# A recurrent attention block in front of two MLPs: another order for the first block, fewer products for the key grams, other kinds of products for the joins

## The chip, the cores and the metric

The kernel runs on one core of a Trainium2 chip. The metric is device time in microseconds. One core has five engines that run side by side and meet only at semaphores: TensorE (PE) multiplies matrices, VectorE (DVE) and ScalarE (ACT) work elementwise and empty PSUM, GpSimd (POOL) does a few elementwise jobs, SyncE (SP) issues the DMAs.

## The reference, cut to what matters

Attention with a delta rule over 768 steps for 32 (batch, head) pairs with head dimension 48, then two MLPs of 384 by 2048, the first with ELU, the second with a sigmoid gate.

```python
k_n = k / (norm(k, axis=-1) + 1e-06)
for t in range(S):
    y[:, :, t] = einsum('bhd,bhde->bhe', q[:, :, t], state)
    v_old = einsum('bhde,bhd->bhe', state, k_n[:, :, t])
    state = state + beta[:, :, t] * einsum('bhd,bhe->bhde', k_n[:, :, t], v[:, :, t] - v_old)
x = y.transpose(0, 2, 1, 3).reshape(B * S, H * D)
h = x @ w_in                                   # first MLP
x = where(h > 0, h, exp(minimum(h, 0)) - 1) @ w_out
h = x @ w_in2                                  # second MLP
out = (h * sigmoid(1.702 * h)) @ w_out2
```

## The kernel before, in words

The 768 steps are cut into six blocks of 128 tokens (`p`, 0 to 5), each of two chunks of 64 (`c = 2p` and `2p + 1`). Within a chunk the recurrence is solved by the inverse of a triangular matrix that is built from the products of the keys.

Two kinds of work share PE. The MLPs run as 192 *units*: two layers, six blocks of tokens, 16 slices `m` of the hidden dimension. A unit's nine products into `h` (`up`, L699) give 128 hidden values for 512 tokens; two units later nine products into `acc` (`down`, L736) take them further. Both kinds are fp32r, 512 columns wide, with each operand split in a high and a low part. The attention of block p+1 is laid between the units of block p of the first layer. Only the attention of block 0 has nothing to hide behind: it stands in front of the first unit and is called the *head* here. Its end is the first row of L699.

The attention's steps, with the names that the text uses:

- **gram** (L196 in later blocks, L210 in the first two): products of the keys of a chunk, into PSUM tile `ps_w`, from there to `z` in SBUF. L196 makes them in pieces of 32 rows, so that the two halves of each row piece come out already swapped; one ACT copy (L202) empties them.
- **inverse**: a chain of small VectorE steps (`take`, `root`, `norm` with L300, `scale` L304, 14 `rows` of L320 and L325 each, `finish`, `turn`). `also(n)` puts n steps of block 1's inverse between the steps of the head; what is left of them goes into the first units by `spread`.
- **join** (`join16`; `left` L360 or L376, `right` L360 or L389): puts the inverses of 16 by 16 together to 32 by 32, in products of 64 by 64 with a block-diagonal operand (`pairs`, L360) or in four times as many of 32 by 32 or 16 by 32 (L376, L389). `block` (L345) copies the block-diagonal operand.
- **kq**, **mask** (L492), **t2**, **m1** (L508), **m2** (L523, L434), **ks** (L539), **w** (L556), **state** (L579), **y** (near part L604, far part L614): the rest of a chunk, in this order of need. `state` of a chunk feeds `ks` of the next one, `ks` feeds `w`, and `y` gives the MLP's input `xh`, `xl`.
- **weight steps** (`bases` L658, `conv`: shift L665, rest L668, cast L675, low L679): turn a loaded slice of weights into its high and low part. Unit m needs slice m.

All of it is a manual schedule: every engine runs its instructions in the order in which the code issues them, and waits in place. `ps_w` is a single PSUM tile of two banks, so each use of it waits until the one before has been copied out. In the unit loop the places of a unit are called `fill` (behind ACT's first two operations), `mid` (ahead of the unit's second VectorE operation) and `end` (behind the cast L721 of the unit); a *slot* 2u is mid of unit u, 2u + 1 is its end. Weight slice m + 2 stands in `fill` of unit m.

Of the kernel before, what the change touches and what calls it, by code (L numbers as in the profile page):

```python
# [31 lines left out]
class Kernel:  # L32
# [34 lines left out]
    def constants(self):  # L67
# [6 lines left out]
        for c in range(2):  # L74
            t = self.wp.tile([P, 2 * DM, 2], F32, name="raw", tag="wt").rearrange("p k i -> p (k i)")[:, 0:1024]
            nc.gpsimd.memset(t, 0.0)
            self.blocks.append(t.rearrange("p (u t) -> p u t", u=16))
# [15 lines left out]
        for k in range(2):  # L93
            for turn in range(2):
                t = self.ap.tile([P, 2, HS], F32, name=f"su{k}{turn}")
                nc.gpsimd.memset(t, 0.0)
                self.su[k, turn] = t
        self.x1d = self.dp.tile([NP, P, NK, TB], F32, name="x1d")
# [83 lines left out]
    def gram(self, c, kt, ps=None):  # L182

        s = self.pas[c // 2]
        if ps is None:
            both = self.wide()
            ps = [both[:, hf] for hf in range(2)]
# [9 lines left out]
        z = s["z"][:, 16 * (c % 2):16 * (c % 2) + 16, :].rearrange("p (f u) t -> p f (u t)", f=2)  # L197
        if c < 2:
            self.nc.scalar.copy(z[:, 0], ps[0])
            self.nc.vector.tensor_copy(z[:, 1], ps[1])  # L200
        else:
            self.nc.scalar.copy(z, both)  # L202

    def gram64(self, c, kt, ps):
# [6 lines left out]

        z = self.pas[c // 2]["z"][:, 16 * (c % 2):16 * (c % 2) + 16, :]
# [134 lines left out]
    def join16(self, c, home):  # L347
# [5 lines left out]
        wide = [c < 4, 0 < c < 4]  # L353

        def pairs(ps, x, half):

            for u in range(8 * half, 8 * half + 8):
                for o in (0, 64):
                    r = slice(o, o + 64)
                    pe.matmul(ps[r, u, :], own["d"][r, u, :], x[r, u, :], start=True, stop=True)  # L360
# [5 lines left out]
        def left(half):  # L366
# [3 lines left out]
            if wide[0]:  # L370
                own["d"] = self.blocks[c % 2 if c < 2 else 1 - c % 2]
                pairs(ps, s["zt"][:, us, 16:32], half)
# [7 lines left out]
        def right(half):  # L380
# [3 lines left out]
            if wide[1]:  # L384
                pairs(ps, own["ys"], half)
# [8 lines left out]
        def blocked():  # L394
            if wide[1]:
                own["d"] = self.blocks[0 if c == 1 else 1 - c % 2]
                self.block(own["d"], own["t1"])
# [45 lines left out]
    def chunk(self, c):  # L443
# [144 lines left out]
        def y():  # L588
            self.x_tiles(("a", c // 2))
            xh, xl = self.x["a", c // 2]  # L590
            if self.early:
                ps = [self.bank(True) for _ in range(2)]
            else:
                both = self.wide()
                ps = [both[:, i] for i in range(2)]
            for i in range(2):
                for ab in range(2):
                    t = 64 * (2 * i + ab)
                    for hf in range(2):
                        k = self.w_half(hf, ab)  # L600
                        for j in range(4):
                            u = 4 * i + j
                            d = 64 * u + 16 * (u % 2)
                            pe.matmul(  # L604
                                ps[0][32 * j:32 * j + 32, 256 * hf + t:256 * hf + t + 64], su[k][:, hf, d:d + 32],
                                g["x"][k][:, 8 * hf + u, :], start=True, stop=True,
                            )
                    for odd in range(2):
                        for hf in range(2):
                            k = self.w_half(hf, ab)  # L610
                            for j in range(2):
                                u, r = 4 * i + 2 * j + odd, 64 * hf + 32 * j
                                d = 64 * u - 16 if odd else 64 * u + 32
                                pe.matmul(  # L614
                                    ps[1][r:r + 32, t:t + 64], su[k][:, hf, d:d + 32], g["x"][k][:, 8 * hf + u, :],
                                    start=not odd, stop=odd == 1,
                                )
            dst = slice(256 * (c % 2), 256 * (c % 2) + 256)
            if self.early:
                pieces = [(slice(0, 2), ps[0]), (slice(2, 3), ps[1][:, 0:256])]  # L620
            else:
                pieces = [(slice(0, 3), both.rearrange("p i t -> p (i t)")[:, 0:768])]
            for r, src in pieces:
                src = src.rearrange("p (k t) -> p k t", t=256)
                act.copy(xh[:, r, dst], src)
# [563 lines left out]
```

## Time and profile before

| | us |
|---|---|
| median of 3 runs | 994.9 (994.07 to 996.52) |
| profiled execution | 994.21 |
| its span, first to last instruction | 992.5 |
| PE busy | 951.7 (96%) |
| DVE busy | 598.2 (60%) |
| ACT busy | 455.6 (46%) |

The shares are means over unlike stretches. From 200 us on PE is busy to within one or two per cent in every stretch; in front of the first unit (73.4 us) it is not, and DVE and ACT are busier there than later. A wait that counts is one of PE behind the head, or one on the chain that leads up to the first unit.

### The profile page before, as it was taken

Reading aid. Unit: us, or ns where it says so; the run is one execution under the profiler, and the core shown is the slowest. Engines: PE = TensorE matmul, PEld = TensorE weight load, DVE = VectorE, ACT = ScalarE, POOL = GpSimd, SP = SyncE. Lnnn points to the kernel's source line nnn. Section 1 sums busy time; section 2 is a strip of 40 time slices with the busy share of each in tenths; the row PEclk is TensorE's granted clock in tenths of the full one; section 3 lists DMA queues with packets and bytes.
Section 4 is the critical chain, followed back from the end, with each engine's and each line's share of the span. In section 5 each row is a group of like instructions: output and inputs, shape, how many; then the busy total and the mean of one; then the engine's idle time right before and its main releaser. Section 6 shows DMA issues by size and latency. Waiting matters only on the chain.

```text
span 992.5 us, 26270 instructions
## 1 busy us (share of the span) xinstructions
PE 951.7 (96%) x11840; PEld 782.4 (79%) x11840; DVE 598.2 (60%) x1038; ACT 455.6 (46%) x754; POOL 80.2 (8%) x71
## 2 busy tenths in 40 slices
PE   4689979999999999999999999999999999999998
PEld 4677767878878887887887888888888888888886
DVE  6878789577886887886445766733333333333332
ACT  6556656443445445444446675533333233333322
POOL 3112222010001001000000100100001001010000
PEclk9999989999999999999999999999999999999999
DMA  7154341502312130210104901010010010100000
GB/s 229 78 194 146 99 144 41 171 5 78 96 56 77 54 98 19 85 51 34 35 19 158 396 1 64 1 40 25 0 64 1 1 64 1 64 0 1 33 1 32
DMA packets 20177, 68.38 MB, mean 69 GB/s; under 512 B 3168, under 2 KB 4704, under 8 KB 20064
## 3 DMA queue, kind: packets, MB, share of 16 engines
q1 hardware_dynamic: 19920, 66.56, 19.6%
q8 instruction: 93, 1.52, 0.6%
q14 instruction: 20, 0.16, 0.1%
q10 hardware_dynamic: 144, 0.13, 0.0%
HBM read 57.25 MB, written 9.44 MB: 67 GB/s over the span
## 4 chain that ended last, share of the span: by engine, by line
PE 88%; DVE 5%; ACT 3%; issue 2%; DMA 1%; POOL 0%; SPq 0%; ACTq 0%; POOLq 0%; DVEq 0%
PE h L699 39%; PE acc L736 28%; PE accn L736 10%; PE ps_w L196 1%; PE ps_w L481 1%; PE ps_w L539 1%; PE ps_b L360 1%; PE ps_w L604 1%; PE ps_w L556 1%; PE ps_w L614 1%; DVE w L665 1%; DMA kg<-in_kT 1%; PE ps_w L579 1%; DVE w L668 1%; PE ps_w L434 1%
## 5 line engine op out<-in xcount | busy, mean ns | idle before, releaser
L699 PE MATMUL h<-xh,wt 128*128 128x512 f32 x1152 | 394.2, 396 | 1.2 <-DVE xl L626 1.2
L736 PE MATMUL acc<-gh,wt 128*128 128x512 f32 x864 | 293.2, 394 | 0.5 <-DVE xo L797 0.5
L699 PEld LDWEIGHTS h<-xh,wt 128*128 128x128 f32 x1152 | 217.0, 188 | 49.4 <-DVE xl L626 1.4
L699 PE MATMUL h<-xl,wt 128*128 128x512 f32 x576 | 225.1, 391 | 0.0
L721 ACT CAST gh<-t 128x512 fp32r<-128x512 f32 x192 | 119.3, 621 | 181.1 <-DVE t L712 125.0
L736 PEld LDWEIGHTS acc<-gh,wt 128*128 128x128 f32 x864 | 163.0, 189 | 36.1 <-issue 1.4
L724 DVE TENSOR_TENSOR gl<-t,gh 128x512 fp32r<-128x512 f32 x192 | 138.6, 722 | 71.4 <-ACT gh L721 71.3
L736 PE MATMUL acc<-gl,wt 128*128 128x512 f32 x432 | 169.0, 391 | 0.0
L718 DVE TENSOR_TENSOR t<-t,h 128x512 f32<-128x512 f32 x96 | 66.0, 688 | 168.8 <-ACT t L715 168.7
L715 ACT ACTIVATE t<-h 128x512 f32<-128x512 f32 x96 | 57.5, 599 | 187.3 <-PE h L699 187.3
L699 PEld LDWEIGHTS h<-xl,wt 128*128 128x128 f32 x576 | 108.7, 189 | 21.1
L712 DVE SCALAR_TENSOR_TENSOR t<-t,h 128x512 f32<-128x512 f32 x96 | 65.7, 684 | 65.4 <-ACT t L709 65.0
L708 ACT ACTIVATE t<-h 128x512 f32<-128x512 f32 x96 | 57.5, 598 | 89.6 <-PE h L699 88.9
L736 PE MATMUL accn<-gh,wt 128*128 128x512 f32 x288 | 96.4, 389 | 0.0
L736 PEld LDWEIGHTS acc<-gl,wt 128*128 128x128 f32 x432 | 81.6, 189 | 16.2
L736 PEld LDWEIGHTS accn<-gh,wt 128*128 128x128 f32 x288 | 54.1, 188 | 11.2
L709 ACT ACTIVATE t<-t 128x512 f32<-128x512 f32 x96 | 60.7, 632 | 3.1
L763 POOL TENSOR_TENSOR xl<-x1r,xh 128x512 fp32r<-128x512 f32 x18 | 24.1, 1337 | 408.3 <-ACT xh L762 314.4
L736 PE MATMUL accn<-gl,wt 128*128 128x512 f32 x144 | 56.0, 389 | 0.0
L492 DVE TENSOR_TENSOR x<-ps_w,mask_p 64x512 f32<-64x512 f32 x44 | 30.2, 687 | 12.6 <-PE ps_w L481 12.1
L679 POOL TENSOR_TENSOR wt<-w,wt 128x768 fp32r<-128x768 f32 x16 | 29.4, 1841 | 65.8 <-ACT wt L675 65.7
L668 DVE SCALAR_TENSOR_TENSOR w<-raw,w 128x768 uint32<-128x768 uint32 x32 | 33.7, 1053 | 0.9
(181 smaller groups left out, 857.6 us busy)
## 6 DMA issues: line engine op xcount, KB each, us to landing
raw<-in_w SPq DMA_DIRECT2D x32, 768.0 KB, 7.7
kt<-in_kT SPq DMA_DIRECT2D x12, 512.0 KB, 4.3
x<-in_qT SPq DMA_DIRECT2D x24, 256.0 KB, 4.1
kg<-in_kT SPq DMA_DIRECT2D x9, 512.0 KB, 5.0
kn<-in_kn SPq DMA_DIRECT2D x12, 384.0 KB, 3.5
x1d<-xo SPq DMA_DIRECT2D x12, 384.0 KB, 2.9
x1r<-x1d SPq DMA_DIRECT2D x6, 768.0 KB, 4.7
vn<-in_vn SPq DMA_DIRECT2D x11, 384.0 KB, 3.6
```

Source lines behind the costliest of these rows:

```text
L492: v.tensor_tensor(out=g["x"][k][self.tok(k), 8 * hf:8 * hf + 8], in0=i, in1=self.mask_p[t].unsqueeze(1).to_broadcast(list(i.shape)), op=AL ...
L668: v.scalar_tensor_tensor(out=bits[m], in0=words(m, 0), scalar=29, in1=bits[m], op0=ALU.logical_shift_right, op1=ALU.bitwise_or)
L679: (v if layer else nc.gpsimd).tensor_tensor(out=wt[:, 1], in0=bits.pop(m).bitcast(F32), in1=wt[:, 0].bitcast(F32), op=ALU.subtract)
L699: nc.tensor.matmul(hps, wt[:, part, k * P:(k + 1) * P], src[:, k], start=(i == 0), stop=(i == 3 * NK - 1))
L708: nc.scalar.activation(out=t, in_=hps, func=AF.Relu, scale=-1.0)
L709: nc.scalar.activation(out=t, in_=t, func=AF.Exp, scale=-1.0)
L712: nc.vector.scalar_tensor_tensor(out=t, in0=t, scalar=-1.0, in1=hps, op0=ALU.add, op1=ALU.max)
L715: nc.scalar.activation(out=t, in_=hps, func=AF.Sigmoid, scale=1.702)
L718: nc.vector.tensor_tensor(out=t, in0=t, in1=hps, op=ALU.mult)
L721: nc.scalar.copy(gh, t)
L724: nc.vector.tensor_tensor(out=gl, in0=t, in1=gh.bitcast(F32), op=ALU.subtract)
L736: self.nc.tensor.matmul(self.acc[c], wt[:, part, DM + c * P:DM + (c + 1) * P], src, start=(m == 0 and i == 0), stop=(m == NM - 1 and i == 2),)
```

## The change

Five edits.

1. **Gram of blocks 2 to 5**: 32 products of 64 rows instead of 64 of 32 rows. The halves now come out unswapped, so two more ACT copies of 32 partitions by 1024 (L192 of the changed kernel) swap them on the way out.
2. **Joins**: chunk 0's right part becomes a product by pairs like the other three of block 0 (a third block-diagonal operand, four more small ACT copies). Chunks 2 and 3 go the other way: four times as many small products, and no block copies.
3. **Head**: another order of the same steps. All four masks of chunk 0 move ahead of block 1's `take`; chunk 0's right join comes ahead of the weight steps; 13 of block 1's 23 inverse steps stand in the head instead of 21; the state of chunk 0 goes into `acc` banks instead of `h`.
4. **y in two parts**: `ya` and `yb`. In the head the near part of chunk 0's y stands ahead of ks of chunk 1, the far part behind it.
5. **Slots in the units**: the grams of block 2 move from end of units 1 and 3 to mid of units 0 and 1, state of chunk 1 from mid of unit 0 to mid of unit 2, most steps of chunks 2 and 3 one or two slots back; y of chunk 2 from mid of unit 9 to mid of unit 10; the first gram of block 3 from end of unit 13 (right behind y of chunk 3) to end of unit 14.

```diff
-    def gram(self, c, kt, ps=None):
...
-        for u in range(8):
-            for hf, ab in self.order():
-                r = 64 * self.s_half(hf, ab)
-                k = kt[r:r + D, 8 * hf + u, :]
-                o = ps[hf][:, 64 * u:64 * u + 64]
-                turned = kt[r:r + D, 8 * hf + u, :].rearrange("p (a b) -> p a b", a=2)[:, ::-1]
-                for sub, x in ((0, k), (1, turned)):
-                    q = 64 * ab + 32 * sub
-                    self.nc.tensor.matmul(o[q:q + 32], k[:, 32 * sub:32 * sub + 32], x, start=True, stop=True)
...
+    def gram(self, c, kt):
+
+        both = self.wide()
+        self.gram_products(kt, [both[:, hf] for hf in range(2)])
+        z = self.pas[c // 2]["z"][:, 16 * (c % 2):16 * (c % 2) + 16, :]
+        x = both.rearrange("p f (u t) -> p (f u) t", u=8)
+        self.nc.scalar.copy(z, x)
+        for r in (slice(32, 64), slice(96, 128)):
+            self.nc.scalar.copy(z[r].rearrange("p u (a b) -> p u a b", a=2), x[r].rearrange("p u (a b) -> p u a b", a=2)[:, :, ::-1])
+
+    def gram_products(self, kt, ps):
...
                 self.nc.tensor.matmul(ps[hf][64 * ab:64 * ab + 64, 64 * u:64 * u + 64], k, k, start=True, stop=True)
...
-        wide = [c < 4, 0 < c < 4]
+        wide = [c < 2, c < 2]
...
             if first:
-                ps = [self.bank(True) for _ in range(2)]
+                ps = self.banks(0)
...
+        run(j0[0], j1[0])
+        run(j0[3], j0[1], j0[2])
+        run(j1[1], j1[3], j1[2])
+        c0["mask"]()
+        also(2)
+        run(j0[4], j0[5], bases[0], c0["t2"])
+        also(1)
+        run(bases[1], c0["m1"], conv[0], conv[1], c0["nv"])
+        run(j1[4], j1[5], c1["t2"])
+        run(c0["m2"], c1["mask"], c1["m1"], conv[2], c0["ks"], c0["w"], conv[3])
+        run(bases[2], c1["m2"], c1["nv"])
+        c0["state"]()
...
+        also(2)
+        run(c0["ya"], c1["ks"], c0["yb"], bases[3])
+        also(2)
+        run(conv[4], c1["w"])
         nc.scalar.activation(out=self.one, in_=self.one, func=AF.Exp)
...
+        also(6)
+        run(c1["ya"], c1["yb"])
...
-            spread(fill, 0, 2, [f for _, f in beside], [size for size, _ in beside])
+            spread(fill, 0, 3, [f for _, f in beside], [size for size, _ in beside])
...
-                self.passes(at, spread, end, fill, p, (1, 3), (6, o + 2), lambda: turned(2))
+                self.passes(at, spread, (mid, end), fill, p, (0, 2), (6, o + 2), lambda: turned(2))
```

What moved, at two places that the prediction speaks of. VectorE between chunk 1's w and the first unit, before (L563 copies chunk 1's w, L320 and L325 are rows of block 1's inverse, L626 writes the first unit's `xl`, L329 to L336 finish the inverse, L665 and L668 prepare weight slice 2):

```order
L563 COPY su_93<-acc_1028 64x8x48
L320 TENSOR_TENSOR tmp<-W 128x72
L325 TENSOR_TENSOR W<-W,tmp 128x2x3x12
...
L626 TENSOR_TENSOR xl<-h,xh 128x2x256
L626 TENSOR_TENSOR xl<-h,xh 128x256
L329 MEMSET W 128x32
L330 TENSOR_TENSOR W<-W,f 128x1024
L336 STREAM_TRANSPOSE xl<-W 128x32x32
L665 TENSOR_SCALAR w<-raw 128x768
L668 SCALAR_TENSOR_TENSOR w<-raw,w 128x768
```

The same stretch in the changed kernel (L297 is `scale`, L554 the copy of w, L313 and L318 the rows, L624 `xl`, L682 and L685 weight slice 2):

```order
L297 TENSOR_TENSOR W<-W,na 128x1024
L554 COPY su_90<-acc_975 64x8x48
L554 COPY su_94<-acc_975 64x8x48
L313 TENSOR_TENSOR tmp<-W 128x28
...
L624 TENSOR_TENSOR xl<-h,xh 128x2x256
L624 TENSOR_TENSOR xl<-h,xh 128x256
L313 TENSOR_TENSOR tmp<-W 128x112
...
L318 TENSOR_TENSOR W<-W,tmp 128x2x3x12
L682 TENSOR_SCALAR w<-raw 128x768
L685 SCALAR_TENSOR_TENSOR w<-raw,w 128x768
```

`scale` now stands in front of the copy of w, six rows stand between that copy and `xl`, and six more between `xl` and weight slice 2; the finish of the inverse is behind that slice.

ScalarE in the unit that holds the first gram of block 2, before (unit 1: L675 casts a weight slice, L721 casts `gh`, L202 empties the gram, L658 and L653 belong to later slices, L708 and L709 open the next unit):

```order
L675 CAST wt<-w 128x768
L721 CAST gh<-t 128x512
L202 COPY z<-ps_w 128x1024
L658 ACTIVATE raw<-raw 128x768
L653 COPY raw<-one 128x1
L708 ACTIVATE t<-h 128x512
L709 ACTIVATE t<-t 128x512
```

In the changed kernel (unit 0: L692 casts the weight slice, L190 and L192 empty the gram, L738 casts `gh`, L675 and L670 belong to later slices, L725 and L726 open the next unit):

```order
L692 CAST wt<-w 128x768
L190 COPY z<-ps_w 128x1024
L192 COPY z<-ps_w 32x1024 x2
L738 CAST gh<-t 128x512
L675 ACTIVATE raw<-raw 128x768
L670 COPY raw<-one 128x1
L725 ACTIVATE t<-h 128x512
L726 ACTIVATE t<-t 128x512
L692 CAST wt<-w 128x768
```

Three copies stand ahead of the cast of `gh` where one stood behind it, and the second gram's three copies follow one unit later.

## Rows read from the trace of the kernel before

**Rows 1.** The page: busy time with instruction counts; the instruction queue (packets, MB, share).

```profile
PE 951.7 (96%) x11840; PEld 782.4 (79%) x11840; DVE 598.2 (60%) x1038; ACT 455.6 (46%) x754; POOL 80.2 (8%) x71
...
q8 instruction: 93, 1.52, 0.6%
```

**Rows 2.** Waits of PE: us in total, times, longest.

```profile
PE ps_w L614 <- issue: 4.4, 1, 4.4
...
PE ps_w L196 <- DVE xl L626: 2.4, 1, 2.4
```

**Rows 3.** Timeline of PE, head and first units: start, us, instruction [idle before].

```profile
28.55 3.60 PE L360 MATMUL h<-xl,raw 64*64 64x16 f32 x64 [3.13 <-DVE xl L336]
...
53.50 2.02 PE L579 MATMUL h<-su,kn 64*48 64x48 f32 x64
...
57.87 2.45 PE L539 MATMUL ps_w<-su,kt 48*64 48x48 f32 x64 [0.51 <-ACT su L795]
...
73.41 0.50 PE L699 MATMUL h<-xh,wt 128*128 128x512 f32 x1 [1.22 <-DVE xl L626]
...
90.28 1.16 PE L481 MATMUL ps_w<-x,kt 48*64 48x64 f32 x64
...
93.64 2.04 PE L360 MATMUL ps_b<-xh,raw 64*64 64x16 f32 x64
...
97.88 1.58 PE L196 MATMUL ps_w<-kg 48*32 48x64 f32 x128
99.39 0.50 PE L699 MATMUL h<-xh,wt 128*128 128x512 f32 x1
```

**Rows 4.** Timeline of DVE, head and unit 0.

```profile
20.98 0.28 DVE L325 TENSOR_TENSOR W<-W,tmp 128x112 f32<-128x112 f32 x1
...
38.47 0.42 DVE L392 TENSOR_TENSOR z<-xl,h 128x256 f32<-128x256 f32 x1
...
42.22 0.18 DVE L300 TENSOR_SCALAR na<-f 128x32 f32<-128x32 f32 x1
...
45.14 1.23 DVE L304 TENSOR_TENSOR W<-W,na 128x1024 f32<-128x1024 f32 x1
...
76.96 0.55 DVE L665 TENSOR_SCALAR w<-raw 128x768 uint32<-128x768 uint32 x1
77.54 0.96 DVE L668 SCALAR_TENSOR_TENSOR w<-raw,w 128x768 uint32<-128x768 uint32 x1
```

**Rows 5.** Groups of ACT by form: busy us, mean ns of one, idle before.

```profile
L721 ACT CAST gh<-t 128x512 fp32r<-128x512 f32 x192 | 119.3, 621 | 181.1 <-DVE t L712 125.0 <-DVE t L718 55.7
L709 ACT ACTIVATE t<-t 128x512 f32<-128x512 f32 x96 | 60.7, 632 | 3.1
...
L708 ACT ACTIVATE t<-h 128x512 f32<-128x512 f32 x96 | 57.5, 598 | 89.6 <-PE h L699 88.9
L658 ACT ACTIVATE raw<-raw 128x768 f32<-128x768 f32 x32 | 28.8, 909 | 0.4 <-DMA raw<-in_w 0.2
L675 ACT CAST wt<-w 128x768 fp32r<-128x768 f32 x32 | 26.4, 825 | 9.8 <-DVE w L668 9.8
...
L437 ACT ACTIVATE z<-ps_w 32x1024 f32<-32x1024 f32 x10 | 10.2, 1018 | 5.7 <-PE ps_w L434 5.6
L202 ACT COPY z<-ps_w 128x1024 f32<-128x1024 f32 x8 | 8.1, 1012 | 3.0 <-PE ps_w L196 3.0
```

**Rows 6.** Timeline of ACT in the head.

```profile
57.35 0.97 ACT L795 COPY su<-h 48x384 f32<-48x384 f32 x2
58.22 1.20 ACT L528 ACTIVATE z<-ps_b 32x512 f32<-32x512 f32 x2
```

**Rows 7.** Timeline of PE: behind chunk 2's y, and a join by quarters.

```profile
141.87 0.48 PE L614 MATMUL ps_w<-x,su 128*32 128x64 f32 x9 [4.41 <-issue]
...
209.49 1.26 PE L389 MATMUL ps_b<-w 16*32 16x16 f32 x128
```

**Rows 8.** Windows: us, busy (x) of PE, PEld, DVE, ACT, POOL, granted clock, DMA share, GB/s.

```profile
142.00:146.00 4.00, 4.00 (x18) 3.06 (x17) 2.86 (x5) 1.99 (x3) 0.00 (x0) 0.50 0.02 4
```

More of the change, by code (lines that the diff above doesn't have):

```diff
@@ L97, in constants @@
                 self.su[k, turn] = t
+        nc.gpsimd.memset(self.blocks[2], 0.0)
         self.x1d = self.dp.tile([NP, P, NK, TB], F32, name="x1d")
@@ L370, in left @@
             if wide[0]:
-                own["d"] = self.blocks[c % 2 if c < 2 else 1 - c % 2]
-                pairs(ps, s["zt"][:, us, 16:32], half)
+                pairs(ps, self.blocks[c], s["zt"][:, us, 16:32], half)
             for u in range(8 * half, 8 * half + 8 * (not wide[0])):
@@ L384, in right @@
             if wide[1]:
-                pairs(ps, own["ys"], half)
+                pairs(ps, self.blocks[2 - 2 * c], own["ys"], half)
             for u in range(8 * half, 8 * half + 8 * (not wide[1])):
@@ new lines, in y_near @@
+        def y_near(i):
+            ps = st["y"]
+            for ab in range(2):
+                t = 64 * (2 * i + ab)
+                for hf in range(2):
+                    k = self.w_half(hf, ab)
+                    for j in range(4):
+                        u = 4 * i + j
+                        d = 64 * u + 16 * (u % 2)
+                        pe.matmul(
+                            ps[0][32 * j:32 * j + 32, 256 * hf + t:256 * hf + t + 64], su[k][:, hf, d:d + 32],
+                            g["x"][k][:, 8 * hf + u, :], start=True, stop=True,
+                        )
@@ L618, in y, with y_out @@
-            dst = slice(256 * (c % 2), 256 * (c % 2) + 256)
+                                ps[1][r:r + 32, t:t + 64], su[k][:, hf, d:d + 32], g["x"][k][:, 8 * hf + u, :],
+                                start=not odd, stop=odd == 1,
+                            )
+        def y_out(r, src):
+            xh, xl = self.x["a", c // 2]
+            dst = slice(256 * (c % 2), 256 * (c % 2) + 256)
+            src = src.rearrange("p (k t) -> p k t", t=256)
+            act.copy(xh[:, r, dst], src)
+            v.tensor_tensor(out=xl[:, r, dst], in0=src, in1=xh[:, r, dst].bitcast(F32), op=ALU.subtract)
@@ L619, in y, with ya @@
+        def ya():
+            y_tiles()
+            y_near(0)
             if self.early:
-                pieces = [(slice(0, 2), ps[0]), (slice(2, 3), ps[1][:, 0:256])]
-            else:
[L622 to L625, printed above, removed]
-                v.tensor_tensor(out=xl[:, r, dst], in0=src, in1=xh[:, r, dst].bitcast(F32), op=ALU.subtract)
@@ L628, in chunk, with yb @@
-        return dict(nv=nv, t2=t2, m1=m1, kq=kq, mask=mask, m2=m2, ks=ks, w=w, state=state, y=y)
+                y_near(1)
+                y_out(slice(0, 2), st["y"][0])
+            else:
+                y_far(0)
+        def yb():
+            if self.early:
+                y_far(0)
+                y_far(1)
+                y_out(slice(2, 3), st["y"][1][:, 0:256])
+            else:
+                y_near(1)
+                y_far(1)
+                y_out(slice(0, 3), st["both"].rearrange("p i t -> p (i t)")[:, 0:768])
@@ L960, in schedule @@
             f()
-        c1["ks"]()
-        c0["y"]()
         also(2)
-        c1["w"]()
-        also(3)
-        c1["y"]()
-        self.block(self.blocks[0], z1[:, 16:32])
+        run(c0["ya"], c1["ks"], c0["yb"], bases[3])
+        also(2)
+        run(conv[4], c1["w"])
+        nc.scalar.activation(out=self.one, in_=self.one, func=AF.Exp)
+        also(6)
+        run(c1["ya"], c1["yb"])
         self.early = False
```

133 lines of the change are left out of this document (40 added, 93 removed), and 6 rows, old and new, of the table z1.

## The prediction, made before the result was known

> **What bounds the kernel now.** Read the busy shares first: PE is busy for 951.7 of 992.5 us [rows 1], and behind the first units it is the engine that the others wait for. So an edit is worth something in three ways only: less work in PE's stream, a wait less of PE, or an earlier first unit. The list of PE's waits, read next, has two that matter behind the first units: 4.4 us inside chunk 2's y and 2.4 us in front of a gram [rows 2]. In the head PE's timeline shows blocks of 64 records at about 2 us (L579, L539) where the like takes 1.16 at 90 us (L481) [rows 3], half the pace, with gaps between. There a chain through PE, ACT and DVE sets the end. Two marks serve below: unit 0 starts at 73.41 us, unit 4 at 99.39 [rows 3].
>
> **The head: 4.0 us earlier.** Up to 28.55 us the order is the same. Then PE runs left of chunk 0, left of chunk 1 and, new, right of chunk 0 by pairs, three blocks of 3.60 us [rows 3]: 39.35. The four new block copies, the masks and `take` lie under these on ACT and DVE; the third operand's memset is POOL's, 20 us before it is needed. The subtraction, 0.42 [rows 4], and m1, some 1.9 like the other 64-record blocks, give 41.7; right of chunk 1, 3.6: 45.3; m2 of chunk 0, m1 of chunk 1, w, m2 of chunk 1 and state, five blocks of 1.9 to 2.0: 54.8. Before, state started at 53.50 and took 2.02 [rows 3]. Its copies wait on ACT behind a weight step, 0.91 [rows 5], and m2's two copies, 1.20, and take 0.97 [rows 6]: 56.95. The near part of y, new here, fills PE meanwhile. ks, 2.0 of its 2.45 behind the first wait, started at 57.87 before [rows 3]; now it ends at 59.0, the far part of y, a 64-record block again, at 60.8, w of chunk 1 at 62.8. Now VectorE is late: six norm steps from 0.18 upward, 1.5 with their gaps, and the scale, 1.23 [rows 4], stand ahead of its half of the copy of w. That half ends at 65.5, and y of chunk 1, which starts on ACT's half, at 68.5. Six rows of the inverse, twelve instructions of up to 0.28 [rows 4], 3.2 with gaps, stand ahead of `xl`, which ends at 69.4. Unit 0 gets going there.
>
> **Units 0 to 3: 2.3 us of it are given back.** Behind `xl` VectorE has six more rows, 3.8, then 0.55 and 0.96 for weight slice 2 [rows 4]: 74.7. ACT casts that slice, 0.83, before it may empty the gram, with one copy of 1.01 and two of 32 partitions by 1024 with their halves swapped [rows 5]. The trace has no such copy; it lies between 0.62, a 512-column cast, and twice the 1.02 of L437, and I take 1.02, which is its shape [rows 5]. That gives 78.6. PE, through unit 1's products at 74.6, waits that long for `ps_w`. ACT goes on in its queue, 0.62 + 0.91 + 0.60 + 0.63 + 0.83 [rows 5] and a small copy, to 82.4, and empties the second gram: 85.5. Only then may state of chunk 1 write `ps_w`; PE, through unit 2 at about 82, waits again. The second gram's keys, loaded behind the first gram, land under the first wait; weight slices are asked for six units ahead and don't feel that load in front of them on SP's queue. From 85.5 PE is the bound: state, 0.9; two `acc` blocks and one of h, 2.27 each; two joins at 1.2 and kq at 1.1: unit 4 at 96.7, 2.7 us ahead of 99.39. Long waits cost clock too: behind the 4.41 us gap [rows 7] the four microseconds from 142 ran at a granted clock of 0.50, the lower of its two levels [rows 8], so 2.0 us were lost. Here most of that would fall into the second wait; I take 1.0, within 0 to 4. Lead at unit 4: 1.7 us.
>
> The extra ACT copies of later grams cost nothing: ACT is busy 46% [rows 1], and a whole unit of PE covers them until `ps_w` is used again. Without that cover they would cost what they cost here.
>
> **Less work behind unit 4: 4.1 us.** A gram was 128 records in 1.58; the new form has the shape of kq, 64 records in 1.16 [rows 3]. Six grams at 0.42: 2.5. A join by pairs takes 2.04 for 64 records [rows 3], by quarters 1.26 for 128 [rows 7]; the two joins of chunk 3 at 0.78: 1.6. The bounds are nothing, if a piece ends at a wait, and about twice that.
>
> On the joins a rule speaks against the change. The row shows 128 records in 1.26 us, 10 ns apart [rows 7]. The Trainium skill (TensorE: Matmul & The Clock Gate, Wait — 56ns, not 53.3ns?) says that matmuls start no closer than some 25 ns however small they are; by that, as an estimate, a join of 128 takes 3.2 us and the four joins cost 4.6 more than before, not 3.1 less. The measured row decides here.
>
> **Waits that go: 1.2 us.** The 2.4 us in front of block 3's first gram [rows 2] were the emptying of chunk 3's y, with one `acc` block between; now a whole unit lies between. But y of chunk 2 (mid of unit 10) and ks of chunk 3 (end of unit 10) now stand as close as those two did, where a whole unit lay between. Between nothing and 2.4 I take half.
>
> **The 4.4 us gap: 3.0 us.** It cuts a row of 16 equal products in two [rows 7], with nothing to wait for. The instruction queue moved 1.52 MB in 93 packets, for 23,680 records of PE [rows 1]: about 128 products with their weight loads in each. Counted off at that rate in the order, a packet border lies at the gap and the one before it in unit 9, 3.5 us of PE's work earlier and about 9 us before the gap's end. I read the gap as PE waiting for its next packet while weights are being loaded. In the new order a border falls into the same y, but with 7.1 us of work in front of it. Of 4.4 us and 2.0 for the clock, 2 to 3 would stay; the next border follows 3.8 us of work later and may cost as much again. Between 0 and 6.4 I take 3.0.
>
> The trace shows PE idle there for 4.41 us [rows 7]. The Trainium skill (Runtime: NRT & Kernel Launch, Instruction fetch mechanics) has instructions come in blocks of 256, the size found here, and calls the fetch mostly hidden. If it is hidden here, the gap has another cause and stays: 3.0 us more in the sum, which the range holds.
>
> **Sum.** 994.2 (the profiled execution's own time) − 1.7 − 4.1 − 1.2 − 3.0 = 984.2. The median before is 0.7 above that execution, so I forecast 985 us. The new turns of y and ks and of m2 and ks in later blocks move work between places where PE shows no wait: nothing, plus or minus one.
>
> **Rivals.**
>
> *No packet gap and no wait behind y.* 994.2 − 1.7 − 4.1 − 2.4 − 6.4 = 979.6, carried over 980. For it: the gap is a single one behind the first units. Against: the next border follows close.
>
> *The units give all of the lead back.* If PE comes out of the two waits at the lower clock and stays there into unit 3, the lead at unit 4 is gone; if the packet gap and the y wait stay as well, only the 4.1 are left: 990, carried over 991. For it: the chain through ACT is made of measured rows. Against: from 85.5 on nothing but PE is late.
>
> *Slower: packet gaps in units 3 to 5.* Counted off in the same way, three borders in a row lie there 3.2 to 3.6 us of work apart, where before they lay 4.4 to 6.8 apart, and weights are loaded in these units. Each gap like the one before costs 6.4 with its clock. One takes the forecast to 991, two to 998: it decides from the second on. Against: before, a border after 2.8 us of work cost nothing.
>
> *Quarter joins cost by the record.* At the pace of kq's records, 18 ns, 128 take 2.3 us, at that of the pairs, 32 ns, 4.1 [rows 3]. With 3.2, the middle, four joins end 7.8 us above the forecast: 993. Against it stands the row at 209 us [rows 7]; for it, elsewhere, the skill's 25 ns.
>
> **How the numbers follow.** The forecast has 0.56 (its own range 981 to 989), no gap 0.17, the lead given back 0.15, packet gaps 0.09, joins by the record 0.03. About 3 us, 0.3%, is what a measurement of this kernel tells from no change, so 991.9 to 997.9 counts as the same. Faster takes the forecast, the first rival and two thirds of the second: 0.83. The same takes the rest of the second, single gaps and the joins: 0.09. Slower: 0.08. The range is 978 to 992: below it lies a third of the first rival, above it the gaps and the joins.
>
> **What would show it.** Unit 0 near 69 us; a wait of PE of about 4 us in front of the second gram and one of about 3.5 in front of state of chunk 1, both ended by ACT's copies; unit 4 at 96 to 98; grams at 1.16, joins of chunks 2 and 3 at 1.26; no wait in front of block 3's first gram, up to 2.4 in front of ks of chunk 3; the gap in chunk 2's y at 2 us or gone. The forecast is wrong if unit 4 starts later than 99.4, or if gaps without a releaser add up to more than 7 us behind it.

## The result: 0.65% slower, and the profile after

The changed kernel takes 999.6 us (median of 11 runs, 998.5 to 1001.1), the kernel before 992.0 (11 runs, 988.8 to 996.5): 1.0065 times as long, 95% interval 1.0048 to 1.0082. The forecast was 985, in a range of 978 to 992. It had started from 994.9, the median of three runs of the kernel before: it had the change at 9.9 us of gain, and 7.6 us of loss came. The profiled execution took 999.6 as well, in a span of 997.9. Below, "before" and "after" are the two kernels.

The page says that PE had less to do and lost time all the same, as against [rows 1]:

```profile
PE 949.3 (95%) x11520; PEld 779.3 (78%) x11520; DVE 592.7 (59%) x1038; ACT 466.1 (47%) x758; POOL 81.8 (8%) x72
...
q8 instruction: 90, 1.47, 0.6%
```

2.4 us of work are gone, 7.8 us of idle time came. PE's timeline answers to [rows 2, 3, 7]. A row has its start, its us, the instruction and the number of its matmul records, and in brackets PE's idle time before it and what ended it; `<-issue` stands where the profile shows nothing that PE waited for, and such a stop is called a gap below:

```profile
28.39 3.60 PE L353 MATMUL h<-xl,raw 64*64 64x16 f32 x64 [4.46 <-DVE xl L329]
...
57.26 0.31 PE L530 MATMUL ps_w<-su,kt 48*64 48x48 f32 x2 [1.97 <-ACT su L812]
...
63.96 1.41 PE L547 MATMUL acc<-raw,z 64*64 64x48 f32 x41 [2.49 <-issue]
...
70.71 1.38 PE L613 MATMUL h<-x,su 128*32 128x64 f32 x41 [1.77 <-issue]
72.02 0.80 PE L716 MATMUL h<-xh,wt 128*128 128x512 f32 x1
...
76.14 1.16 PE L200 MATMUL ps_w<-kg 48*64 48x64 f32 x64
...
81.73 1.16 PE L200 MATMUL ps_w<-kg 48*64 48x64 f32 x64 [2.16 <-ACT z L192]
...
88.29 0.94 PE L570 MATMUL ps_w<-su,kn 64*48 64x48 f32 x64 [1.55 <-ACT z L192]
...
98.33 1.26 PE L381 MATMUL ps_b<-xh 16*32 16x16 f32 x128
99.52 0.50 PE L716 MATMUL h<-xh,wt 128*128 128x512 f32 x1
...
148.61 1.15 PE L530 MATMUL ps_w<-su,kt 48*64 48x48 f32 x64 [2.36 <-DVE xl L624]
...
194.94 1.58 PE L381 MATMUL ps_b<-w 16*32 16x16 f32 x128 [2.78 <-DVE w L357]
196.45 0.80 PE L716 MATMUL h<-xh,wt 128*128 128x512 f32 x1
...
285.38 0.47 PE L753 MATMUL acc<-gh,wt 128*128 128x512 f32 x1 [1.03 <-DVE xo L814]
...
292.32 1.16 PE L472 MATMUL ps_w<-x,kt 48*64 48x64 f32 x64 [1.28 <-ACT z L192]
```

Read it from the top. The joins take 3.60, ks gets going at 57.3, and until 60.6 us the head runs as forecast. Then two pieces of 64 records (L547 is w, L613 the far part of y of chunk 1) are cut behind record 23, by gaps that nothing released, and unit 0 starts at 72.0, not 69.4. The two gaps lie 128 records apart: 41 of w, 64 of the near part of y, 23 of its far part. The ten microseconds from 60 ran at a granted clock of 0.50, the lower of its two levels (window: us, busy (x) of PE, PEld, DVE, ACT, POOL, granted clock, DMA share, GB/s):

```profile
60.00:70.00 10.00, 5.68 (x177) 4.70 (x167) 7.37 (x24) 4.19 (x7) 0.00 (x0) 0.50 0.84 266
```

In before the same window had a DMA share of 0.85, one gap of 1.62 us and a granted clock of 1.00.

Unit 4 starts at 99.52, against 99.39 [rows 3]: no lead is left. Behind it stand waits that before did not have. How far a unit's first activation on ACT stands behind that of before (us, minus is ahead; profiled executions) shows where. Of the kernels tried below, "new gram" and "quarter" are before with one part of the change, "late raw" is after with the weight loads later, "late 3-5" after with late copies in blocks 3 to 5, and "three mends" has these two and one more:

```
unit  before |  after | new gram | quarter | late raw | late 3-5 | three mends
   0   75.80 |  +0.45 |   -0.84  |  +0.79  |  -2.59   |  -0.19   |  -2.52
   4  101.77 |  +0.12 |   +2.48  |  -0.78  |  -2.64   |  -0.65   |  -1.65
   9  134.97 |  +2.76 |   +0.68  |  +1.68  |  +0.47   |  +2.34   |  +0.90
  13  164.72 |  -2.08 |   -3.53  |  -2.72  |  -2.76   |  +0.46   |  -2.35
  18  193.01 |  -3.10 |   -0.99  |  +0.17  |  -3.79   |  -0.45   |  -3.25
  20  206.24 |  +0.86 |   -1.72  |  +0.50  |  -1.77   |  -0.92   |  -3.88
  29  259.75 |  +0.77 |   -1.82  |  +0.44  |  -1.86   |  -0.91   |  -3.67
  38  309.00 |  +4.87 |   +2.79  |  +0.44  |  +2.21   |  +1.54   |  -2.80
  54  394.83 |  +6.72 |   +4.65  |  +0.53  |  +4.05   |  +0.87   |  -3.48
```

After loses 4.0 us between units 18 and 20 and 5.9 between units 29 and 54. All columns gain between units 9 and 13, where before has its gap of 4.41 us [rows 7]. Single executions scatter there too: after and late 3-5 have the same code up to unit 14 and stand 2.5 us apart at unit 13.

### The profile page after: what moved, and what is told of

Same layout as the page of the kernel before. It is cut to its first block, busy times and chain, and to the rows that moved or that the text cites. A ratio compares the mean times of both kernels' runs of the same rounds, so it can differ in the third digit from the quotient of the medians.

```text
span 997.9 us, 25630 instructions
## 1 busy us (share of the span) xinstructions
PE 949.3 (95%) x11520; PEld 779.3 (78%) x11520; DVE 592.7 (59%) x1038; ACT 466.1 (47%) x758; POOL 81.8 (8%) x72
## 4 chain that ended last, share of the span: by engine, by line
PE 76%; DVE 13%; ACT 6%; issue 3%; DMA 1%; POOL 0%; DVEq 0%; ACTq 0%; POOLq 0%
PE h L716 33%; PE acc L753 24%; PE accn L753 10%; ACT z L192 2%; DVE t L729 1%; DVE W L308 1%; DVE tmp L303 1%; DVE gl L741 1%; PE ps_w L530 1%; DVE tmp L313 1%; PE ps_w L547 1%; DVE x L483 1%; PE ps_w L472 1%; ACT z L190 1%; DVE su L577 1%
## 5 line engine op out<-in xcount | busy, mean ns | idle before, releaser
L738 ACT CAST gh<-t 128x512 fp32r<-128x512 f32 x192 | 119.3, 621 | 186.2 <-DVE t L729 130.0
L725 ACT ACTIVATE t<-h 128x512 f32<-128x512 f32 x96 | 57.4, 598 | 90.7 <-PE h L716 90.2
L726 ACT ACTIVATE t<-t 128x512 f32<-128x512 f32 x96 | 60.7, 632 | 3.1
L685 DVE SCALAR_TENSOR_TENSOR w<-raw,w 128x768 uint32<-128x768 uint32 x32 | 36.3, 1135 | 0.9
```

Source lines behind the costliest of these rows:

```text
L685: v.scalar_tensor_tensor(out=bits[m], in0=words(m, 0), scalar=29, in1=bits[m], op0=ALU.logical_shift_right, op1=ALU.bitwise_or)
L725: nc.scalar.activation(out=t, in_=hps, func=AF.Relu, scale=-1.0)
L726: nc.scalar.activation(out=t, in_=t, func=AF.Exp, scale=-1.0)
L738: nc.scalar.copy(gh, t)
```

## Experiments

Each was timed beside before, whose median was 992.0 to 992.5 in every series. Ratios are to before, with their 95% interval.

### Whose is the loss

**New gram alone**, in before:

```
-  gram(): 64 halves of products, one ACT copy
+  gram(): as in after, 32 whole products, three ACT copies
```

> The kernel before with the new gram alone: 64 fewer products in each of six grams, three ACT copies instead of one. Theory (clearing the tile costs PE waits where a k q product stands half a unit behind the gram): 6 times 0.42 less on PE, 2.5, against two waits of 1.27 before k q in the later blocks and none in the first units, where the next user of the tile stands a whole unit behind: 0.0, between 1 faster and 1 slower than before. Rival (only PE's stream counts): 2.5 faster than before.

Measured: 999.3, 1.0069 (1.0048 to 1.0090). That is nearly the loss of the whole change, from one part that the forecast counted as 2.5 us of gain; neither theory had it. (The kernel has eight such grams; six of them stand behind unit 4.) The rows of this kernel show how, where the finished sums of units 16 to 31 (`acc`) are copied to `xo`, on ACT, DVE and PE:

```profile
278.41 1.01 ACT L188 COPY z<-ps_w 128x1024 f32<-128x1024 f32 x1
279.45 2.02 ACT L190 COPY z<-ps_w 32x1024 f32<-32x1024 f32 x2
281.50 0.60 ACT L704 ACTIVATE t<-h 128x512 f32<-128x512 f32 x1
```

```profile
282.79 0.69 DVE L708 SCALAR_TENSOR_TENSOR t<-t,h 128x512 f32<-128x512 f32 x1 [3.56 <-ACT t L705]
283.40 1.02 DVE L793 COPY xo<-acc 128x512 f32<-128x512 f32 x2
```

```profile
284.23 0.77 PE L732 MATMUL acc<-gh,wt 128*128 128x512 f32 x1 [2.47 <-DVE xo L793]
284.79 0.63 PE L732 MATMUL acc<-gl,wt 128*128 128x512 f32 x1
...
292.17 1.16 PE L477 MATMUL ps_w<-x,kt 48*64 48x64 f32 x64 [0.92 <-ACT z L190]
```

The kernel before at the same place:

```profile
280.26 1.01 ACT L202 COPY z<-ps_w 128x1024 f32<-128x1024 f32 x1
281.16 0.60 ACT L708 ACTIVATE t<-h 128x512 f32<-128x512 f32 x1
...
282.46 0.69 DVE L712 SCALAR_TENSOR_TENSOR t<-t,h 128x512 f32<-128x512 f32 x1 [1.39 <-ACT t L709]
```

Nobody waits for the tile here. The two extra copies stand in ACT's queue ahead of the next unit's activation, which comes 2 us late; DVE, in order, sits 3.56 us instead of 1.39 and copies the finished sums late; PE may not overwrite them, waits 2.47 us, where before has no wait, and its next products run at a granted clock of 0.50 (0.63 us where 0.39 is usual). The second gram then delays kq by 0.92.

Other kernels agree. Between units 29 and 54, where the grams of blocks 4 and 5 stand, after, this kernel and five others below with the same gram at the same places lose 5.9 to 7.6 us.

**Old gram in after**, all else kept:

> The kernel after with the old gram in blocks 2 to 5: 64 more products each, one ACT copy of 1.0 us instead of three of 1.0 each; every place in the order stays. Theory (the time that ACT takes to clear the two-bank tile is what makes PE wait): the waits that end in ACT's second copy go, 2.16 us before the second gram, 1.55 before chunk 1's state, 1.28 and 1.26 before two k q products, 6.2 in all, and six grams cost 0.42 more each on PE, 2.5: 3.7 faster than after, about 996. Rival (PE's own instructions set the time, and a wait that goes reappears as the next one): 2.5 slower than after, about 1002.

Measured: 999.0, 1.0071 (1.0040 to 1.0103), between the two. From unit 29 to 54 its profile lost 1.6 us where after lost 5.9, but PE's gaps had moved with the longer stream: six of over 1 us, 12.0 together, against four and 7.0 in after (three and 8.0 in before), and at unit 4 it already stood 4.6 us behind after. Its profiled execution, 1002.4, is one of its slower ones. It decides nothing by itself.

**Quarter joins alone**, in before:

```
-        wide = [c < 4, 0 < c < 4]
+        wide = [c < 2, c == 1]
-        self.block(self.blocks[1], z1[:, 0:16])     (and blocks[0], z1[:, 16:32])
```

> The kernel before with chunk 2's and 3's joins in quarters as chunk 0's and 1's partners of after have them (the block copies for them dropped, 8 ACT copies less in the head and 8 in the units): 4 half joins of 2.04 us become 1.26. Theory (PE is the bound behind unit 0, and nothing waits in that stretch): 4 times 0.78 less, 3.1 faster than before. Rival (the second inverse and the transposes of chunk 2 and 3 on DVE set the pace of units 1 to 5, so that PE waits for what it saves): 0 to 1 faster than before.

Measured: 994.7, 1.0022 (1.0000 to 1.0045); neither number. The table does not show the 3.1 us: this kernel is 0.8 ahead at unit 4 and 1.7 behind at unit 9, and in unit 5 PE waits 1.83 us for DVE, a wait of the rival's kind that before does not have. The 2.7 us of lead at unit 13 come from another place: behind unit 9 this kernel lacks before's gap of 4.41 us. That lead ends in front of block 3's first gram, where PE arrives earlier than DVE empties chunk 3's y:

```profile
168.75 2.05 PE L196 MATMUL ps_w<-kg 48*32 48x64 f32 x128 [3.63 <-DVE xl L626]
170.73 0.79 PE L699 MATMUL h<-xh,wt 128*128 128x512 f32 x1
```

3.63 us instead of 2.37 [rows 2], and the gram itself then takes 2.05, at a granted clock of 0.50, where it took 1.48 in before: the lead went into the wait and the clock behind it.

**The same with block 3's grams later**, as in after:

```
-                grams = (13, 15) if p == 3 ...      ends of units 13 and 15
+                grams = (14, 16) if p == 3 ...      end of unit 14, middle of 16
```

> The kernel before with the quarter joins of chunks 2 and 3 and block 3's two grams later (end of unit 14 and middle of unit 16 instead of ends of units 13 and 15), as in after. Theory (the quarter joins' 2.5 us were there in units 6 to 13 and were lost at the gram behind chunk 3's y, where PE waited 3.63 us for DVE, against 2.37 in before, and ran at half clock after it): that wait falls below 1 us, the lead stays: 2 to 3 faster than before, 989 to 991. Rival (DVE or the store of block 0's sums sets the time of block 2's first join at unit 18, so that the wait only moves there): 0 to 2 slower than before.

Measured: 991.1, 0.9994 (0.9967 to 1.0020): 3.7 below the quarter joins alone, and not to be told from before. That wait is gone from PE's list.

**Later slots undone.** After with the slots of blocks 3 to 5 as before, and then with the old gram too:

> The kernel after with the slots of blocks 3 to 5 as before: block 3's second product and k s in the old order, its grams one half unit to one unit earlier, y ahead of the second chunk's k s in all blocks, block 2's last y half a unit earlier. Theory (the marks of the units show after losing 4.1 us against before in units 30 to 37, where block 3's stage stands, and 1.9 in units 48 to 53): 4 to 6 faster than after, about 994 to 995. Rival (that stretch loses because of ACT's copies behind the grams, or because DVE comes late from block 2's inverse, and the slots don't matter): 0 to 1 faster.

> The kernel after with the old gram in blocks 2 to 5 and the slots of blocks 3 to 5 as before: what is left of the change is the head's order, the quarter joins and the places of units 0 to 13. So far: new gram alone in before 6.8 slower, quarter joins alone 2.2 slower, after with the old slots 13.2 slower than before. Theory (the new gram is the loss, by ACT's queue, in units 30 to 53; the head by itself gains nothing that lasts): 2 to 3 slower than before, 994 to 996. Rival (the head's order loses by itself, by packet gaps on PE between 60 and 72 us and the half clock behind them): 13.2 less 6.8 = 6 slower, 998 to 1000.

Measured: 1005.7, 1.0127 (1.0078 to 1.0175), and 999.4, 1.0081 (1.0059 to 1.0103). The first missed its theory by 11 us; the second met the rival's number, for another reason. Undone in part, the slots put block 3's first gram straight behind chunk 3's y, which after has half a unit later than before (the first of the two kernels, PE; the second waits 5.10 us there):

```profile
171.88 1.98 PE L200 MATMUL ps_w<-kg 48*64 48x64 f32 x64 [5.09 <-DVE xl L624]
```

So these two price that collision, not the head; after's later slot for the gram belongs to its later y.

**Old head order in after:**

> The kernel after with the head's work in the order of before (bases first, four steps of the second inverse ahead of the joins, y behind k s), block joins, gram, quarter joins and unit slots as in after. Theory A (the head's new order gives unit 0 a start 2 to 4 us earlier where no packet gap falls, and the lead is lost by unit 19 at the latest, where block 2's first transpose waits for the store of block 0's sums): same as after, 998 to 1001. Theory B (the new order loses by itself, by packet gaps and half clock between 60 and 76 us): 3 to 5 faster than after, about 995 to 996.

Measured: 998.7, 1.0067 (1.0041 to 1.0092): theory A. With the rest of the change as it is, the head's order is worth nothing at the end, either way.

### The copies moved

**Late copies**, new gram in before; the two copies behind the next unit's activations, and the grams of blocks 4 and 5 one unit earlier (the last edit):

```
+        def far(): (the two turned copies)
+        self.far = far
+        for g in grams: fill.setdefault(g + 1, []).insert(0, lambda: self.far())
-                ... else (o - 16, o - 14)
+                ... else (o - 17, o - 15)
```

> The kernel before with the new gram, whose two copies of the turned quarters stand behind the next unit's two activations on ACT (ahead of its gh) instead of ahead of them; blocks 4's and 5's grams stand one unit earlier, so that no k q product follows at half a unit. Theory (the new gram costs because its copies hold up the next unit's activations and with them DVE's copies of the finished sums and PE's first acc product): the waits of the kernel with the new gram at once, 2.47 us before acc and 0.92 and 1.28 before k q, are gone, and six grams of 0.42 less each stay: 1 to 3 faster than before, 990 to 992. Rival (it is the time for which the tile or z is held, or the turned copies as such): 3 to 7 slower than before, as with the copies at once.

Measured: 989.4, 0.9988 (0.9964 to 1.0012): 9.9 below the new gram alone, and 2.6 below before, which is not clear of noise. The three waits that the theory named are gone, and the stretch from unit 29 to 54 gains 1.6 us instead of losing 6.5; in unit 2 a wait of 2.08 us for the late copies came. Two things were moved at once, though: all 16 ACT copies, and four of the eight grams.

**In after, all blocks**, then **blocks 3 to 5 only** (block 2's grams as in after), both with the grams of blocks 4 and 5 a unit earlier as well:

> The kernel after with one edit: the two copies of a gram's turned quarters stand behind the next unit's two activations on ACT instead of ahead of them, and blocks 4's and 5's grams one unit earlier. Theory (after's loss is these copies: 6 us in units 30 to 53, and 2.16 and 1.55 of PE's waits in units 1 and 2): 5 to 8 faster than after, 992 to 994, and no wait of PE for ACT's z or for DVE's xo behind unit 30. Rival (the lead of after's head and quarter joins is lost by packet gaps and the store ahead of unit 18 whatever the grams do, and the waits reappear): 0 to 2 faster than after.

> The kernel after with the late copies in blocks 3 to 5 alone (block 2's grams as in after, whose second stands half a unit to a unit behind the first). With late copies in all blocks, units 30 to 68 lost 0.2 us to before instead of 5.9, but units 1 to 3 lost 6 more than after, since the tile was held until the next gram. Theory: both known parts add up, 5 to 6 faster than after, 993.5 to 995. Rival (what is gained in units 30 to 53 is lost elsewhere): 0 to 2 faster than after.

Measured: 998.9, 1.0062 (1.0036 to 1.0088), and 993.1, 1.0006 (0.9984 to 1.0028). The first met the rival's number, but not for its reason: between units 29 and 54 it lost 0.2 us. Block 2's grams stand one unit apart on one tile, and late copies hold it (4.28 and 3.39 us of PE's waits where after has 2.16 and 1.55):

```profile
83.85 1.98 PE L204 MATMUL ps_w<-kg 48*64 48x64 f32 x64 [4.28 <-ACT z L194]
...
93.36 1.35 PE L574 MATMUL ps_w<-su,kn 64*48 64x48 f32 x64 [3.39 <-ACT z L194]
```

With those left alone 6.4 us come back, and units 29 to 54 lose 1.8. ACT's order in that kernel, to hold against the one above:

```profile
272.37 1.02 ACT L190 COPY z<-ps_w 128x1024 f32<-128x1024 f32 x1 [0.30 <-PE ps_w L206]
...
274.55 0.60 ACT L731 ACTIVATE t<-h 128x512 f32<-128x512 f32 x1 [1.17 <-PE h L722]
275.18 0.63 ACT L732 ACTIVATE t<-t 128x512 f32<-128x512 f32 x1
275.84 2.03 ACT L194 COPY z<-ps_w 32x1024 f32<-32x1024 f32 x2
277.89 0.62 ACT L744 CAST gh<-t 128x512 fp32r<-128x512 f32 x1
```

How much of this the order on ACT gives, and how much the earlier gram, was not run apart. An estimate from these rows: the first copy ends at 273.39, so the two others, 2.03 us, would have ended at 275.42 in front of the activation, 0.87 us after its own start at 274.55, and not 2 us late as at the old place. The place is thus part of the gain.

### The gaps without a releaser

**Weight loads later**, in after:

```
-        for f in loads[4:6]: f()        behind load_kn(1)
+        for f in loads[4:6]: f()        behind load_q(3)
-            at(tail, m - 2, *bases[m + 2:m + 3], ...)
+            at(tail, max(m - 2, 1), *bases[m + 2:m + 3])
```

> The kernel after with the loads of weight groups 4 and 5 (two transfers of 768 KB) issued behind the loads of chunk 3's q, some 20 us later, and group 4's and 5's bases on ACT at the end of unit 1. Theory (the two gaps of PE without a releaser in the head, 2.49 us in chunk 1's w and 1.77 in its y, are instruction packets that come late because the 16 DMA engines are busy with these loads): both gaps below 1 us, unit 0 starts at 69 to 70 instead of 72.0; the end 0 to 3 faster, since the lead may be lost later. Rival (the gaps have nothing to do with the load): gaps as in after, unit 0 at 72, no change in the end.

Measured: 997.8, 1.0059 (1.0036 to 1.0082), 1.8 below after; unit 0 starts where the forecast had it:

```profile
60.49 0.89 PE L547 MATMUL acc<-raw,z 64*64 64x48 f32 x23
61.75 1.15 PE L547 MATMUL acc<-raw,z 64*64 64x48 f32 x41 [0.37 <-issue]
...
66.21 2.02 PE L613 MATMUL h<-x,su 128*32 128x64 f32 x64
69.25 0.80 PE L716 MATMUL h<-xh,wt 128*128 128x512 f32 x1 [1.01 <-DVE xl L624]
```

The cut behind record 23 is still there, but costs 0.37 us instead of 2.49, and the second one doesn't show. At unit 0 this kernel is 3.0 us ahead of after, at unit 13 still 0.7 (table).

**Empty products at the start**, 64 and then 32:

```
+        empty = self.wide()[:, 0]
+        for i in range(64):
+            nc.tensor.matmul(empty[0:32, 0:16], (zeros 32x32), (zeros 32x16), start=True, stop=True)
```

> The kernel after with 64 empty products of 32 by 16 on PE at the program's start, where PE waits for the first load; they move every border of 128 products by half. Theory (PE's gaps without a releaser are late packets of instructions, so they stand at these borders): every such gap of after, among them the two of the head at product 23 of a piece, goes from its place, and others come half a packet away from them; the end moves by 1 to 4 us either way, though no work is changed behind 5 us. Rival (the gaps belong to the places in the program): the gaps stay where they are, and the end is the same as after's within 0.5.

> The kernel after with 32 empty products at the program's start. A product of this kind leaves two matmul records, so 64 of them moved the borders by a whole packet of 128 records and left the gaps in their places; 32 move them by half. They take some 3.5 us of PE, which fits ahead of the first load's end at 4.4. Theory (the gaps stand at packet borders): the gaps at records 23 of chunk 1's w and 23 of its y are gone from there, and gaps of 1 to 2.5 us stand 64 records earlier or later while loads run; the end moves by 1 to 4 us either way. Rival (places in the program): the gaps stand where they stood, and the end is within 1 us of after's.

Measured: 1002.6, 1.0110 (1.0084 to 1.0136), and 996.5, 1.0034 (1.0015 to 1.0053). The 64 left 128 records, a whole packet, so both gaps of the head stayed at record 23, and as they took 7.0 us the head began 4.4 us late: that run tells nothing apart. The 32 took 3.59 us and moved the first gram by 1.0, and yet the two pieces run uncut:

```profile
61.60 1.85 PE L547 MATMUL acc<-raw,z 64*64 64x48 f32 x64
67.65 1.95 PE L613 MATMUL h<-x,su 128*32 128x64 f32 x64
70.36 0.50 PE L716 MATMUL h<-xh,wt 128*128 128x512 f32 x1 [0.76 <-DVE xl L624]
```

The gaps go with the count of records, not with the place: packet borders. Counted in records, the four gaps of after lie 128, 766 and 383 apart: once, six times and three times 128, to within two. The end came 3.1 us earlier than after's, but not by the head alone: at unit 13 this kernel is 0.3 us ahead of after, and at unit 20 4.7, since it gains 0.4 us on before between units 18 and 20, where after loses 4.0.

### The join at the store, the sum, and a better kernel

DVE's first transpose for chunk 4 waits, in after, for a buffer that the store of block 0's sums still holds:

```profile
188.07 1.01 DVE L814 COPY xo<-acc 128x512 f32<-128x512 f32 x2
...
194.09 0.71 DVE L357 STREAM_TRANSPOSE w<-kg 128x512 f32<-128x512 f32 x1 [3.35 <-DMA x1d<-xo]
```

In before the same wait was there, and PE had other work:

```profile
195.06 0.71 DVE L364 STREAM_TRANSPOSE w<-kg 128x512 f32<-128x512 f32 x1 [1.57 <-DMA x1d<-xo]
```

**Chunk 4's first join half a unit later** (its right part, and the piece behind it):

```
-        for slot, c, i in ((4, 4, 0), (4, 4, 1), (5, 4, 3), ...
+        for slot, c, i in ((4, 4, 0), (5, 4, 1), (6, 4, 3), ...
```

> The kernel after with chunk 4's first join half a unit later (end of unit 18 instead of its middle). In after PE waited there 2.78 us for a transpose on DVE, whose buffer was held by the store of block 0's sums (3.35 us of DVE's wait), and ran at half clock behind it; the marks of units 18 to 19 lost 3.6 us. Theory (a wait at this place alone): seven products of the second layer stand ahead of the join and take 1.6 us, the wait falls to about 1, the clock stays: 2 to 3.5 faster than after, 996 to 997.5. Rival (PE waits for the same store or for DVE at the next join instead): 0 to 1 faster.

Measured: 997.2, 1.0034 (1.0017 to 1.0051), 2.4 below after, and PE's join no longer waits:

```profile
196.12 1.58 PE L381 MATMUL ps_b<-w 16*32 16x16 f32 x128
```

**Three mends at once** (late copies in blocks 3 to 5, this join, the weight loads):

> The kernel after with three mends at once: late copies behind the grams of blocks 3 to 5 (6.4 faster alone), chunk 4's first join half a unit later (2.4 faster alone), the loads of weight groups 4 and 5 behind chunk 3's q (1.8 faster alone). Theory (three losses in three stretches, each its own): they add, 10.6 faster than after, 988 to 990.5. Rival (a lead is lost again at the next place where PE waits, as the leads of head and quarter joins were): 993 or more.

Measured: 988.5, 0.9966 (0.9947 to 0.9985): 11.1 below after, where the parts alone give 10.6. They add, and units 29 to 54 lose 0.2.

**Candidates on before**: late copies, quarter joins and block 3's later grams; then with the weight loads later too; then with 32 empty products:

> A candidate: the kernel before with the new gram and its late copies (2.6 faster by itself), the quarter joins of chunks 2 and 3, and block 3's grams later (together 1.0 faster by themselves). Theory (the parts act in different stretches: units 30 to 53, and units 6 to 16): their sum, 3 to 4 faster than before, about 988; with the 3.64 us wait before block 3's first gram gone, up to 2 more. Rival (the lead is lost where PE waits for DVE or the store ahead of unit 18): as the late copies alone, 989 to 990.

> The candidate at 985.0 (before with the new gram and late copies, quarter joins, block 3's grams later) with the loads of weight groups 4 and 5 issued behind chunk 3's q. Theory (the 2.13 us gap of PE in chunk 0's y in the head is a packet held up by these loads): the gap is below 1, unit 0 starts 1 to 2 earlier and nothing behind it takes that back: 983 to 984. Rival (the head ends when DVE's inverse steps end, or unit 2 waits for the later weights): 985 to 987.

> The candidate at 981.5 (before with late copies, quarter joins, block 3's grams later and the weight loads later) with 32 empty products at the start, half a packet of matmul records. In it PE stood 4.39 us without a releaser in chunk 2's y, at record 54 of 64 of a piece. Theory (a packet border): that gap is gone from there, the half clock behind it too, gaps of 1 to 2 us come elsewhere while loads run; 2 to 5 faster, 977 to 980, less some 1 us by which the empty products delay the first gram. Rival (the place in the program): the gap stays, 981 to 983.

Measured: 985.0, 0.9948 (0.9917 to 0.9979); 981.5, 0.9887 (0.9855 to 0.9918); 987.5, 0.9942 (0.9919 to 0.9966). The second beats both kernels; the gap of the head that it was meant for fell from 2.13 to 1.33 us, not below 1. In the third the gap of 4.39 us went, and others came, one of 2.45 in the head and one, 1.63 us, in block 3's second product. The second and the third kernel, PE:

```profile
139.66 0.38 PE L614 MATMUL ps_w<-x,su 128*32 128x64 f32 x10 [4.39 <-issue]
```

```profile
70.61 0.33 PE L614 MATMUL h<-x,su 128*32 128x64 f32 x9 [2.45 <-issue]
```

So a packet border can be moved, but where it does harm next was not foreseen.

## Why the prediction was wrong

- **"The extra ACT copies of later grams cost nothing": the step that failed.** It asked who waits for `ps_w`, and found a unit of cover. The copies also stand ahead of the next unit's activations, and there the cover is nothing: the activation comes 2 us late, DVE behind it, and PE waits for the sums (2.47 us with the new gram alone). Cost: after loses 5.9 us between units 29 and 54, where 1.7 were forecast as gained from four grams. 6.4 come back with the copies behind the activations and blocks 4 and 5's grams a unit earlier.
- **The head, 4.0 us.** The chain was right to 60.6 us. The packet borders were counted off behind unit 3 only; two lay in chunk 1's w and y while the DMA engines were 0.84 busy, and cost 4.3 us and the clock. The trace of before has such a gap there as well, 1.62 us in front of the last 9 records of a piece at 64.44 us. With the loads later unit 0 starts at 69.25, forecast 69.4. At the end this is worth 1.8.
- **Units 0 to 3.** Both waits came, ended by ACT's copies: 2.16 and 1.55 us instead of 4 and 3.5. PE came to the first of them 5.0 us later than forecast, at 79.6, and the tile came free 3.1 later, at 81.7. Unit 4 at 99.52 was the sign named as refuting.
- **Less work, 4.1 us.** The new pieces were sized rightly, 1.16 and 1.26 us. The old gram was not: 1.58 is the row of one in the first units, the six that count took 1.48 in before, so they give 1.9 us and not 2.5. The lower bound, a piece that ends at a wait, was the case: in before with the quarter joins at DVE and at the gram behind y, in after at the store. The store's 1.57 us of DVE's wait could be read in the trace of before.
- **Waits, 1.2 us.** Mis-sized: 2.37 us in front of the gram became 0.75, but 2.36 came in front of ks of chunk 3. Together that is 0.7 us lost, outside the bounds of nothing and 2.4 gained.
- **The gap, 3.0 us.** It is gone, and 32 empty products move one like it in another kernel, as a packet border would. 1.49 and 1.21 us came at kq of chunk 3 and at m1 of chunks 2 and 3. By the table after gains 4.8 us on before between units 9 and 13 and loses 2.6 between units 4 and 9.
- **The slower rival.** Its 998 lies near the measured time by luck. It needed two packet gaps in units 3 to 5, and one of over 1 us came there, 1.49.
- Three mends bring 988.5. The last 3.5 us to the forecast were not taken apart.

## What to carry to other kernels

Price an instruction by everything behind it in its engine's queue, not by who waits for its result: two copies per gram behind the activations instead of ahead of them, with four of the eight grams a unit earlier, were worth 6 to 10 us. Before counting a gain on the bounding engine, look for the first place where it meets another engine or a transfer with a small wait now; the gain can end there. A kernel whose profile shows gaps without a releaser can move by 3 us and more when its instruction count changes, so one part's effect is read from its stretch, in more than one kernel, and not from the end.

## What the runs showed of the hardware

Gaps of up to 4.4 us came inside stretches of small products, those of after at distances of 128 records and multiples of it, an instruction packet each by the prediction's count; one such border cost 2.49 us, and 0.37 with two 768 KB loads issued later. The Trainium skill (Runtime: NRT & Kernel Launch, Instruction fetch mechanics) calls this fetch mostly hidden; in these stretches it was not.

The length of a wait did not tell the clock behind it. In front of ks of chunk 3 PE waited 2.3 to 2.4 us in twelve kernels with after's order: in eight its 64 records then took 1.15 us (granted clock 1.00 in after), in four 1.56 to 1.96. With 32 empty products at the start of after the granted clock was 0.50 there:

```profile
145.37 1.96 PE L530 MATMUL ps_w<-su,kt 48*64 48x48 f32 x64 [2.36 <-DVE xl L624]
```

Block 3's first gram took 2.05 us at 0.50 behind a wait of 3.63 (quarter joins alone), and in its new form the usual 1.16 at 1.00 behind 3.64 (late copies in before).

The two 384 KB stores of block 0's sums took a median 5.1 us to land in after, 3.3 in before, 2.8 with chunk 4's join later and 2.3 with the three mends; why was not tried.
